# Softmax sums inverted by VectorE block transposes in all attention groups, a third W3 buffer and a new order table

## The chip, the cores and the metric

The kernel runs on one core of a Trainium2 chip. The metric is device time in microseconds (us) of one execution, taken as the median of several runs. The engines are named as in the profile: PE is TensorE (its weight loads are PEld), ACT is ScalarE, DVE is VectorE, POOL is GpSimd, and SP is SyncE, which here issues every DMA. A profile is one further execution, recorded instruction by instruction; its times are counted from the start of its span.

## The reference

The input is x with 2048 rows and 640 columns in bfloat16. Branch A is attention with 32 heads of 20 columns, branch B is a mixer with an MLP, and the second gates the first.

```python
def reference(A_x, A_wqkv, A_wo, B_x, B_w1, B_w2, B_w3, B_w4):
    def _A_ref(x, wqkv, wo):
        B, S, D = x.shape
        H = 32
        Dh = D // H
        ...
        scores = jnp.einsum("bhqd,bhkd->bhqk", q, k) * (Dh ** -0.5)
        p = _softmax(scores, axis=-1)
        o = jnp.einsum("bhqk,bhkd->bhqd", p, v)
        return (lambda x, *d: x.transpose(*d))(o, 0, 2, 1, 3).reshape(B, S, D) @ wo

    def _B_ref(x, w1, w2, w3, w4):
        h = _gelu(_layernorm(x, axis=-1) @ w1)
        ...
        x1 = x + hs
        h2 = _gelu(_layernorm(x1, axis=-1) @ w3) @ w4
        return x1 + h2

    x = A_x
    xn = _layernorm(x, axis=-1)
    s = _A_ref(xn, A_wqkv, A_wo)
    g = _silu(_B_ref(xn, B_w1, B_w2, B_w3, B_w4))
    return x + s * g
```

The hs left out is four shifted quarters of h times w2. What matters for the change is the softmax: exponentials are summed over the keys, and each head's output is divided by its sum.

## The kernel before

**Groups.** The 32 heads are worked in 8 quads of four heads, and each quad in 4 chunks (qc) of 512 queries: 32 groups, called quad_qc. In a group the four heads lie in four strips of 32 partitions. For every tile of 128 keys PE computes scores into PSUM (`score_act`, `score_rows`, `score_both`; their matmuls are L1377, one head's strip of rows each, and L1392, the same scores in column form). ACT takes the exponential of most of them (L1434, 1024 columns at a time, and L1416, 2048 columns). Some score tiles go to DVE instead, which builds exponentials from bits (L1461 takes scores out of PSUM, L1360 makes three shifted copies). PE then multiplies by the values (L1235 for ACT's tiles, L1369 for DVE's) and accumulates the whole group in one PSUM bank, the PV bank. In each strip rows 0 to 19 of that bank are a head's output, and row 20 is its sum of exponentials, since the values carry a column of ones.

**Normalising.** `normalise` (L1468) ends a group. It is written in two forms. In the last quad (three groups; the very last group is worked in two halves by `last_half`) it stays on DVE: a transpose in 32x32 blocks from the PV bank to the buffer Ob (L1483) brings the sums of 16 blocks side by side in each partition, a reciprocal of 16 columns inverts them (L1485), one tensor_tensor multiplies every block by its reciprocal (L1491), and a second block transpose turns the result back (L1493). In the other 7 quads, 28 groups, the sums go through DRAM. DVE copies the PV bank to Ob (L1496). SP stores the sums of the four heads to the DRAM tensor `sums` (L1499) and loads them back spread over 128 partitions into ZT (L1501). DVE inverts them (L1503). SP stores the reciprocals to `recips` (L1505) and loads them back, each row repeated for 32 partitions, into RB (L1507). DVE multiplies Ob by RB into one half of On (L1509). In both of these forms the next group's PV matmuls wait until Ob has been filled. The 28 groups then store their heads with four DMAs to the DRAM tensor `heads` (L1514), from where `otq` fetches them for the output projection.

**Other work.** Between the attention instructions lie the stacks of keys and queries (`stack`, L1104 to L1143: weights, matmuls in `mm_tile`, L640, evictions L1112, stores L1114), the fetches of the next quad (L1133), the masked queries of a group (`qm`, four DMAs at L1202) and branch B. In `b_w34` each of the 4 chunks streams W3 in 12 tiles of 160 KB into W3s (L1795), 48 loads in all. W3s has two buffers, so a tile's load can go only when the tile two before has been used by PE. W4 is loaded in halves (L1809). The two Gelus of this part are single ACT instructions (L1804); a third belongs to `b_w1` (L1733).

**What sets the order.** Each operation is a task (`T`) with its engine, what it reads and what it writes. The order of all tasks is written out in the string TABLE, and `Planner.follow` replays it: two characters give the number of a task, and one more character follows for each set of slots that it takes (PSUM banks, buffers of exponentials). Each engine runs its own tasks in that order, and waits are put where a task reads or writes what another engine's task made or still uses. SP is in order too: a DMA whose wait is not over holds all DMAs behind it. Score tasks made with `flex` choose row or column form by what PE has before and after them in the table, as these lines say:

```python
                nx = next(later)
                if t.flex and (pe_mode or (nx is not None and (nx.mode or nx.flex))):
                    t.mode, t.dur = 1, self.row_dur
```

Of the kernel before, what the change touches and what calls it, by code (L numbers as in the profile page):

```python
# [436 lines left out]
FP32 = mybir.dt.float32  # L437
# [7 lines left out]
class Handle:  # L445
    _n = 0
# [128 lines left out]
class Gen:  # L575
# [71 lines left out]
    def build(self, plan_only=False):  # L647
        nc, pl = self.nc, self.pl
        with contextlib.ExitStack() as es:
# [4 lines left out]
            self.dz, self.dr = (nc.dram_tensor(n, (2, 4, 512), FP32, kind="Internal").ap() for n in ("sums", "recips"))  # L654
# [113 lines left out]
    def alloc_persistent(self):  # L768
# [28 lines left out]
        self.ZT = self.alloc("ZT", [2, 16], FP32)  # L797
        self.RZ = self.alloc("RZ", [2, 16], FP32)
        self.RB = self.alloc("RB", [512], FP32)
# [387 lines left out]
    def attn_quad(self, quad):  # L1187
# [9 lines left out]
        for qc in range(NQC):  # L1197
            seq = cfg.order(quad, qc)
            gb = self.grp % 2
# [47 lines left out]
    def last_half(self, quad, qc, half, gb):  # L1247
# [40 lines left out]
        for x, kt in enumerate(ks):  # L1288
            hs, sa = scores(kt, "a")
            hp, pa = self.exp_act(hs, sa)  # L1290
# [89 lines left out]
    def score_act(self, b, qc, kt, a, gb=None):  # L1380
# [4 lines left out]
        def fn(e):  # L1385
            for jj in range(2):
# [4 lines left out]
                for c in range(4):  # L1391
# [5 lines left out]
                    writes=[sa], name=f"sc{self.step}", mode=int(gb is None), part=a + 1, flex=gb is not None, cls=-1, acq=("S", hs)))  # L1397
        return self.exp_act(hs, sa)

    def score_rows(self, b, qc, kt, wide):  # L1400
# [3 lines left out]
        def fn(e):  # L1404
# [4 lines left out]
          writes=[a for _, a in tiles], name=f"sr{self.step}", mode=1, cls=-1, acq=("SW" if wide else "SR",) + tuple(h for h, _ in tiles))  # L1409
        if not wide:  # L1410
            return [self.exp_act(h, a) for h, a in tiles]
# [6 lines left out]
          reads=[a0, a1], writes=pa, name=f"exp{self.step}", due=self.at(self.nact + 2), acq=("PT2", hp[0], hp[1]), rel=[h0, h1], cls=0)  # L1418
# [10 lines left out]
    def exp_act(self, hs, sa):  # L1429
        cfg = self.cfg  # L1430
        hp = Handle()
        pa = ("PT", hp.id)
        self.T("act", c_act(1024),
               lambda e: e.activation(self.PT[:, hp.slot, :], self.psum[:, 512 * hs.slot:512 * hs.slot + 1024], AF.Exp, scale=cfg.scale),  # L1434
               reads=[sa], writes=[pa], name=f"exp{self.step}", due=self.at(self.nact + 1), acq=("PT", hp), rel=hs)
        self.step += 1
        self.nact += 1
        return hp, pa

    def score_both(self, b, qc, kt, a, quad, r):  # L1440
# [9 lines left out]
        def fn(e):  # L1450
# [5 lines left out]
          name=f"sb{self.step}", mode=1, cls=-1, acq=("SD", hs, hd))  # L1456
        slot = self.exp_act(hs, sa)
# [10 lines left out]
    def normalise(self, quad, qc):  # L1468
# [9 lines left out]
        else:  # L1478
            dst, dsta = self.On[:, ob, :], [A("On", ob)]
        if last:  # L1480
            OnT = self.On[:, ob, :]
            cls = -1
            T("dve", c_dve(512), lambda e: e.transpose(Ob[:, :], self.bank(self.PVB)[:, :]),  # L1483
              writes=[("PV", 0), A("Ob")], name=f"ob{quad}_{qc}", cls=cls)
            T("dve", c_dve(16, "recip"), lambda e: e.reciprocal(RZ[:, ob, 0:16], Ob[:, 20:512:32]),  # L1485
              reads=[A("Ob")], writes=[A("RZ", ob)], name=f"rz{quad}_{qc}", cls=cls)
            def fnn(e):
                in0 = Ob[:, :].rearrange("p (a b) -> p a b", b=32)
                r = RZ[:, ob, 0:16]
                in1 = bass.AP(r.tensor, r.offset, [list(r.ap[0]), [1, 16], [0, 32]])  # L1490
                return e.tensor_tensor(OnT[:, :].rearrange("p (a b) -> p a b", b=32), in0, in1, op=ALU.mult)  # L1491
            T("dve", c_dve(512, "1x"), fnn, reads=[A("Ob"), A("RZ", ob)], writes=[A("On", ob)], name=f"onT{quad}_{qc}", cls=cls)
            T("dve", c_dve(512, "1x"), lambda e: e.transpose(dst, OnT[:, :]), reads=[A("On", ob)], writes=dsta, name=f"on{quad}_{qc}", cls=cls)  # L1493
            return
        ZT, RB = self.ZT, self.RB
        T("dve", c_dve(512), lambda e: e.tensor_copy(Ob[:, :], self.bank(self.PVB)[:, :]),  # L1496
          writes=[("PV", 0), A("Ob")], name=f"ob{quad}_{qc}", cls=-1)
        dz, dr, do = self.dz, self.dr, self.do
# [452 lines left out]
```

## Time and profile before

| what | us |
|---|---|
| median of 3 runs | 866.87 |
| the 3 runs | 865.56, 868.62, 866.87 |
| the profiled execution, device time | 864.35 |
| its span from first to last instruction | 862.6 |
| exponentials on ACT, L1434, 788 instructions | 733.1 |
| score evictions on DVE, L1461, 245 instructions | 264.8 |
| shifted copies on DVE, L1360, 174 instructions | 195.7 |

A row of the groups of instructions names the line, the engine and the operation, then output and input with their shapes, the number of instructions, their busy time in us and the mean length of one in ns, and after a bar the idle time of the engine just before them with what ended it. In the timeline the first two numbers are start and length in us, and square brackets give idle time before the instruction and what ended it. SPq is SP issuing a DMA. The chain of waits follows the work that ended last back to the start, so its shares say through which engine the end was reached.

### The profile page before, as it was taken

What the parts mean: (1) busy time and instruction counts of PE and PEld (TensorE: products, weight loads), DVE (VectorE), ACT (ScalarE), POOL (GpSimd) and SP (SyncE); (2) the same over time, 40 slices, a digit from 0 to 9 for tenths busy, and PEclk for the clock granted to TensorE, in tenths of its full rate; (3) what the DMA queues carried; (4) which work ended last, traced back from release to release, by engine and by line L of the source; (5) the groups of instructions that cost most, each with busy time, mean ns of one, the idle gap of its engine ahead of it and who ended that gap; (6) DMA issues with size and microseconds to landing.
All of it is one profiled execution on the core that took longest, in us unless ns stands there. A gap on an engine that the chain in (4) does not pass through costs nothing.

```text
span 862.6 us, 32161 instructions
## 1 busy us (share of the span) xinstructions
PE 802.2 (93%) x14614; PEld 338.8 (39%) x14614; DVE 719.2 (83%) x1005; ACT 815.6 (95%) x854; POOL 39.2 (5%) x75
## 2 busy tenths in 40 slices
PE   7999999899999999989999999999897899989996
PEld 4433333334345433333434444343233344433475
DVE  7549998998998899979887899988785788997765
ACT  7799999999999999989999999999799999999996
POOL 5610000000000000000000000000000000010000
PEclk9999999999999999999999999999998999999999
DMA  7002453331210023222223121322212102031232
GB/s 230 17 2 65 110 125 107 77 98 47 62 53 17 24 73 89 66 57 63 66 66 86 30 61 41 94 59 79 56 44 57 48 26 71 25 106 63 81 106 79
DMA packets 86472, 58.88 MB, mean 68 GB/s; under 512 B 53056, under 2 KB 77840, under 8 KB 86336
## 3 DMA queue, kind: packets, MB, share of 16 engines
q1 hardware_dynamic: 86336, 56.82, 24.4%
q8 instruction: 115, 1.88, 0.9%
q14 instruction: 21, 0.17, 0.1%
HBM read 42.10 MB, written 10.63 MB: 61 GB/s over the span
## 4 chain that ended last, share of the span: by engine, by line
ACT 46%; PE 35%; DVE 11%; DMA 5%; SPq 2%; issue 1%; DVEq 0%
ACT arena L1434 42%; PE psum L640 13%; PE psum L1392 6%; PE psum L1377 5%; PE psum L1369 4%; DVE arena L1461 4%; PE psum L1235 3%; DMA arena<-in_B_w_dram 3%; DVE arena L1360 2%; PE psum L1276 2%; ACT arena L1804 1%; ACT arena L1733 1%; DMA arena<-sums 1%; ACT arena L1820 1%; DVE arena L855 1%
## 5 line engine op out<-in xcount | busy, mean ns | idle before, releaser
L1434 ACT ACTIVATE arena<-psum 128x1024 bf16<-128x1024 f32 x788 | 733.1, 1041 | 27.9 <-PE psum L1377 19.5
L640 PE MATMUL psum<-arena 128*32 128x320 bf16 (+1 forms) x5952 | 364.8, 334 | 8.6 <-DMA arena<-in_B_w_dram 5.0
L1461 DVE TENSOR_SCALAR arena<-psum 128x1024 uint16<-128x1024 f32 (+1 forms) x245 | 264.8, 1091 | 41.3 <-PE psum L1377 39.7
L640 PEld LDWEIGHTS psum<-arena 128*32 128x32 bf16 x5952 | 147.1, 96 | 145.0 <-issue 32.0
L1360 DVE TENSOR_SCALAR arena<-arena 128x4096 uint16<-128x4096 uint16 (+1 forms) x174 | 195.7, 1149 | 4.0 <-PE psum L1369 2.6
L1392 PE MATMUL psum<-arena 128*32 128x512 bf16 x2496 | 190.5, 382 | 1.5 <-ACT arena L1434 0.8
L1377 PE MATMUL psum<-arena 32*128 32x512 bf16 x1360 | 160.1, 386 | 29.3 <-ACT arena L1434 21.5
L1369 PE MATMUL psum<-arena 128*22 128x512 bf16 x1728 | 152.5, 385 | 5.0 <-DVE arena L1360 4.9
L1235 PE MATMUL psum<-arena 128*22 128x512 bf16 x1552 | 148.0, 382 | 2.5 <-ACT arena L1434 2.4
L1377 PEld LDWEIGHTS psum<-arena 32*128 32x128 bf16 x1360 | 40.9, 91 | 168.8 <-ACT arena L1434 101.0
L1392 PEld LDWEIGHTS psum<-arena 128*32 128x32 bf16 x2496 | 49.2, 95 | 72.0 <-ACT arena L1434 60.0
L1369 PEld LDWEIGHTS psum<-arena 128*22 128x22 bf16 x1728 | 41.7, 92 | 54.8 <-issue 14.6
L1235 PEld LDWEIGHTS psum<-arena 128*22 128x22 bf16 x1552 | 38.7, 91 | 50.1 <-issue 16.1
L1112 DVE CAST arena<-psum 128x512 bf16<-128x512 f32 x40 | 27.2, 686 | 14.7 <-PE psum L640 14.4
L1800 DVE CAST arena<-psum 128x512 bf16<-128x512 f32 x48 | 32.8, 685 | 5.1 <-PE psum L640 5.0
L1584 DVE SCALAR_TENSOR_TENSOR arena<-psum,arena 128x320 bf16<-128x320 f32 x32 | 15.5, 486 | 22.8 <-PE psum L640 22.5
L1174 DVE CAST arena<-psum 128x320 bf16<-128x320 f32 x32 | 15.1, 489 | 15.7 <-PE psum L640 14.4
L855 DVE BATCH_NORM_STATS2 arena<-arena 128x6 f32<-128x320 bf16 x54 | 24.3, 481 | 3.1 <-DMA arena<-in_A_x_dram 3.0
L1815 DVE TENSOR_TENSOR arena<-psum,arena 128x320 bf16<-128x320 f32 x32 | 15.5, 485 | 7.0 <-PE psum L640 6.7
L1804 ACT ACTIVATE arena<-arena 128x12288 bf16<-128x12288 bf16 x2 | 20.9, 10446 | 0.0
L1761 DVE TENSOR_TENSOR arena<-psum,arena 128x320 bf16<-128x320 f32 x32 | 15.2, 481 | 6.8 <-PE psum L640 6.6
L1496 DVE COPY arena<-psum 128x512 f32<-128x512 f32 x28 | 19.1, 682 | 1.1 <-PE psum L929 0.4
(121 smaller groups left out, 347.9 us busy)
## 6 DMA issues: line engine op xcount, KB each, us to landing
arena<-in_B_w_dram SPq DMA_DIRECT2D x48, 160.0 KB, 2.6
arena<-recips SPq DMA_DIRECT2D x28, 256.0 KB
arena<-arena SPq DMA_DIRECT2D x124, 32.0 KB, 1.9
arena<-in_B_w_dram SPq DMA_DIRECT2D x4, 960.0 KB, 6.3
arena<-in_A_x_dram SPq DMA_DIRECT2D x8, 320.0 KB, 6.1
arena<-in_A_x_dram SPq DMA_DIRECT2D x16, 160.0 KB, 2.8
out_dram<-arena SPq DMA_DIRECT2D x16, 160.0 KB, 1.8
heads<-arena SPq DMA_DIRECT2D x112, 20.0 KB
```

Source lines behind the costliest of these rows:

```text
L640: ins = e.matmul(pb[32 * c:32 * c + 32, 0:N], lhsT(k, c), rhs(k, c), start=(k == 0), stop=(stop and k == nk - 1), tile_position=(0, 32 * c))
L855: lambda e, li=li, n=n, hh=hh: e.bn_stats(st[:, li, 6 * hh:6 * hh + 6], xn[:, n, hD * hh:hD * hh + hD]),
L1112: T("dve", c_dve(512), lambda e, h=h, c=c: e.tensor_copy(KS[:, 512 * c:512 * c + 512], self.wbank(h)[:, 0:512]), reads=[wa], writes=[A("KS ...
L1235: ins = e.matmul(pb[32 * i:32 * i + 22, 0:512], VA[:, ql, kts[i // 2], i, :], PT[:, slots[i // 2][0].slot, 512 * (i % 2):512 * (i % 2) + 512],
L1360: T("dve", c_dve(w, "4x"), lambda e, v=v, dst=dst: e.tensor_scalar(dst, U[:, ub, 0:w], EXP_B[v], None, op0=ALU.add), reads=halves, writes= ...
L1369: ins = e.matmul(pb[32 * i:32 * i + 22, 0:512], wv, dst[:, at:at + 512].bitcast(BF16), start=first, stop=final, tile_position=(0, 32 * i))
L1377: return e.matmul(out, self.KT[32 * i:32 * i + 32, b, 128 * kt:128 * kt + 128], self.QT[32 * i:32 * i + 32, b, 512 * qc:512 * qc + 512], s ...
L1392: ins = e.matmul(out[32 * c:32 * c + 32, :], self.KT[:, b, 128 * kt + 32 * c:128 * kt + 32 * c + 32], self.QM[:, gb, 2 * a + jj, :], start ...
L1434: lambda e: e.activation(self.PT[:, hp.slot, :], self.psum[:, 512 * hs.slot:512 * hs.slot + 1024], AF.Exp, scale=cfg.scale),
L1461: ins = e.tensor_scalar(U[:, ub, 1024 * at + 512 * k:1024 * at + 512 * k + w], self.psum[:, 512 * hd.slots[k]:512 * hd.slots[k] + w], a_ex ...
L1800: T("dve", c_dve(512), lambda e, h=h, fc=fc, i=i: e.tensor_copy(GT[:, i, fc, :], self.wbank(h)[:, 0:512]), reads=[wa], writes=at, name=f"g ...
L1804: T("act", 2750 + c_act(2 * FC * 512), lambda e: e.activation(GT[:, :, :, :], GT[:, :, :, :], AF.Gelu_apprx_tanh), reads=gta, writes=gta, ...
```

## The change

All groups now use the form of the last quad. The transposed result of a group needs a buffer of its own: in the 28 groups it is the half of On that the group before used. The DRAM tensors for sums and reciprocals and the buffers ZT and RB are gone, with four DMAs per group. W3s gets a third buffer. TABLE is replaced as a whole, since the numbers of the tasks move; score and exponential tasks also get names made of group, key tile and half, which appear in no instruction.

```diff
-            self.dz, self.dr = (nc.dram_tensor(n, (2, 4, 512), FP32, kind="Internal").ap() for n in ("sums", "recips"))
...
-        self.ZT = self.alloc("ZT", [2, 16], FP32)
         self.RZ = self.alloc("RZ", [2, 16], FP32)
-        self.RB = self.alloc("RB", [512], FP32)
...
+        OnT, ota = (self.On[:, ob, :], A("On", ob)) if last else (self.On[:, 1 - ob, :], A("On", 1 - ob))
+        cls = -1
+        T("dve", c_dve(512), lambda e: e.transpose(Ob[:, :], self.bank(self.PVB)[:, :]),
+          writes=[("PV", 0), A("Ob")], name=f"ob{quad}_{qc}", cls=cls)
+        T("dve", c_dve(16, "recip"), lambda e: e.reciprocal(RZ[:, ob, 0:16], Ob[:, 20:512:32]),
+          reads=[A("Ob")], writes=[A("RZ", ob)], name=f"rz{quad}_{qc}", cls=cls)
+        def fnn(e):
+            in0 = Ob[:, :].rearrange("p (a b) -> p a b", b=32)
+            r = RZ[:, ob, 0:16]
+            in1 = bass.AP(r.tensor, r.offset, [list(r.ap[0]), [1, 16], [0, 32]])
+            return e.tensor_tensor(OnT.rearrange("p (a b) -> p a b", b=32), in0, in1, op=ALU.mult)
+        T("dve", c_dve(512, "1x"), fnn, reads=[A("Ob"), A("RZ", ob)], writes=[ota], name=f"onT{quad}_{qc}", cls=cls)
+        T("dve", c_dve(512, "1x"), lambda e: e.transpose(dst, OnT), reads=[ota], writes=dsta, name=f"on{quad}_{qc}", cls=cls)
         if last:
...
             return
-        ZT, RB = self.ZT, self.RB
-        T("dve", c_dve(512), lambda e: e.tensor_copy(Ob[:, :], self.bank(self.PVB)[:, :]),
-          writes=[("PV", 0), A("Ob")], name=f"ob{quad}_{qc}", cls=-1)
-        dz, dr, do = self.dz, self.dr, self.do
-        T("sp", C_SP, lambda e: e.dma_start(dz[ob], Ob[20:128:32, :]), reads=[A("Ob")], writes=[("dz", ob)], is_dma=True, nbytes=8192,
...
-        T("sp", C_SP, lambda e: e.dma_start(ZT[:, ob, :], dz[ob].rearrange("i (a b) -> (i a) b", b=16)), reads=[("dz", ob)],
...
-        T("dve", c_dve(16, "recip"), lambda e: e.reciprocal(RZ[:, ob, :], ZT[:, ob, :]),
...
-        T("sp", C_SP, lambda e: e.dma_start(dr[ob].rearrange("i (a b) -> (i a) b", b=16), RZ[:, ob, :]), reads=[A("RZ", ob)],
...
-        T("sp", C_SP, lambda e: e.dma_start(RB[:, :], bass.AP(dr.tensor, dr[ob].offset, [[512, 4], [0, 32], [1, 512]])),
...
-        T("pool" if cfg.ONP else "dve", 1500 if cfg.ONP else c_dve(512, "1x"), lambda e: e.tensor_tensor(dst, Ob[:, :], RB[:, :], op=ALU.mult),
...
+        do = self.do
...
-        self.W3s = self.alloc("W3s", [2, KC, 128], BF16)
+        self.W3s = self.alloc("W3s", [3, KC, 128], BF16)
...
-                ws = self.w3k % 2
+                ws = self.w3k % 3
```

## The prediction

> **What bounds the kernel now.** I read the page's totals first, then busy time by stretch, then the chain of waits, then the timeline around its longest DMA pieces.
>
> ```profile
> span 862.6 us, 32161 instructions
> PE 802.2 (93%) x14614; PEld 338.8 (39%) x14614; DVE 719.2 (83%) x1005; ACT 815.6 (95%) x854; POOL 39.2 (5%) x75
> ...
> ACT 46%; PE 35%; DVE 11%; DMA 5%; SPq 2%; issue 1%; DVEq 0%
> ```
>
> ScalarE (ACT) is the bound: 815.6 of 862.6 us busy, so all its idle time is 47 us, and no change that leaves its work alone can gain more. The third line, the chain that ended last, still passes through DVE for 11% and DMA for 5%. The stretches say where the idle 47 us lie (columns: length, then busy us of PE, PEld, DVE, ACT, POOL):
>
> ```profile
> 0.00:44.00 44.00, 37.98 (x858) 19.61 (x862) 29.54 (x99) 32.82 (x53) 26.47 (x50) 1.00 0.42 121
> 44.00:160.00 116.00, 109.88 (x1714) 39.49 (x1706) 96.71 (x119) 110.59 (x119) 2.80 (x7) 1.00 0.33 84
> 160.00:300.00 140.00, 133.14 (x2452) 56.71 (x2452) 124.11 (x193) 137.86 (x139) 2.90 (x6) 1.00 0.19 52
> 300.00:450.00 150.00, 142.82 (x2402) 54.38 (x2398) 134.46 (x176) 144.43 (x144) 4.07 (x9) 1.00 0.26 66
> 450.00:650.00 200.00, 187.70 (x3310) 76.24 (x3310) 173.09 (x207) 191.71 (x205) 0.00 (x0) 0.99 0.25 63
> 650.00:760.00 110.00, 101.68 (x1870) 43.90 (x1862) 88.69 (x105) 107.79 (x104) 0.00 (x0) 0.97 0.16 44
> 760.00:863.00 103.00, 89.00 (x2040) 48.49 (x2036) 72.63 (x112) 90.37 (x95) 2.94 (x3) 0.96 0.29 91
> ```
>
> Start and end hold 11.2 and 12.6 us, and the change leaves the work of both alone. The middle, 44 to 760, where the 28 changed groups run, holds 5.4 + 2.1 + 5.6 + 8.3 + 2.2 = 23.6 us of ACT idle. That is what can be won there. DVE is busy 617 of these 716 us: 99 us are free, but all in pieces.
>
> The largest single piece of ACT idle in the middle starts on the SP queue:
>
> ```profile
> 603.47 0.34 SPq L1505 DMA_DIRECT2D recips<-arena  x1
> 606.78 0.59 SPq L1507 DMA_DIRECT2D arena<-recips  x1
> 607.42 10.82 SPq L1795 DMA_DIRECT2D arena<-in_B_w_dram  x3
> ...
> 612.82 0.68 PE L640 MATMUL psum<-arena 128*32 128x512 bf16 x8 [2.59 <-DMA arena<-in_B_w_dram]
> ...
> 614.40 1.02 ACT L1434 ACTIVATE arena<-psum 128x1024 bf16<-128x1024 f32 x1 [3.04 <-PE psum L1392]
> ```
>
> SP works in order. It sends the reciprocals out (L1505, 603.47) and waits until they are in DRAM before it fetches them back (L1507, 606.78). The W3 tile (L1795) queued behind leaves only at 607.42 and is awaited by PE, which stands for 2.59 us; ACT runs dry 3.04 us. The same order (L1507 at 375.87, L1795 at 376.51) precedes a PE stop of 1.58 us at 381.69 and an ACT gap of 1.66 us at 383.43.
>
> [...] 8 KB from L1501 or L1505 lands after 2.2 us in the median, and L1507 held SP for 41.7 us in all waiting for L1505's data. [...] L1509 takes 682, L1491 688. [...] the last quad's transposes, 705 and 706 ns, cost about what the 682 ns copy of the same size does. So every new DVE operation has a measured row.
>
> **The change, part by part.** All sums are made against the profiled span, 862.6 us; its own time was 864.35 and the median of the three others is 866.87, so I apply the difference to 866.87.
>
> 1. DVE. The old group is L1496 + L1503 + L1509, the new one L1483 + L1485 + L1491 + L1493, which quad 7 already runs:
>
> ```profile
> L1496 DVE COPY arena<-psum 128x512 f32<-128x512 f32 x28 | 19.1, 682 | 1.1 <-PE psum L929 0.4 <-PE psum L1369 0.3
> L1509 DVE TENSOR_TENSOR arena<-arena 128x512 bf16<-128x512 f32 x28 | 19.1, 682 | 0.0
> L1503 DVE RECIPROCAL arena<-arena 128x16 f32<-128x16 f32 x28 | 6.8, 244 | 3.1 <-DMA arena<-sums 3.1
> ...
> L1483 DVE STREAM_TRANSPOSE arena<-psum 128x512 f32<-128x512 f32 x3 | 2.1, 706 | 0.0
> L1493 DVE STREAM_TRANSPOSE arena<-arena 128x512 bf16<-128x512 bf16 x3 | 2.1, 705 | 0.0
> ...
> L1491 DVE TENSOR_TENSOR arena<-arena 128x512 bf16<-128x512 f32 x3 | 2.1, 688 | 0.1
> ...
> L1485 DVE RECIPROCAL arena<-arena 128x16 f32<-128x16 f32 x3 | 0.7, 247 | 0.1
> ```
>
> Old 682 + 244 + 682 = 1608 ns, new 706 + 247 + 688 + 705 = 2346 ns: 738 ns more, x28 = 20.7 us. The PV bank comes free only 24 ns later (706 against 682). What of 20.7 us lies on the path? Lower end: weight each stretch's groups by DVE's share of the chain there. The chain asked by stretch shows DVE 18.6% (44 to 160, 4 groups), 0 (160 to 300, 6), 8.3% (300 to 450, 5.5), 1.2% (450 to 650, 8.5), 8.6% (650 to 770, 4): 1.65 groups x 0.738 = 1.2 us. Upper end: all, 20.7. A delay off the chain also uses up slack of what follows, so I take three times the lower end, **+3.5 us**.
>
> 2. The trips. Each group loses L1499, L1501, L1505, L1507, 112 DMAs in all, with their SP issue (541 + 350 + 345 + 588 ns = 1.8 us a group) and the waits in front of them. On DVE, L1503 had waited 3.1 us in three stops (100.23, 460.16, 712.02). The first was followed by ACT gaps of 0.80 and 0.76 (102.06, 103.85), the last by 0.21 (713.61), the second by none: **-1.8 us**. I take nothing for the other SP relief (qm, fetch, rstd loads): mostly it lies beside ACT work; between 44 and 160, SP and issue are 11.7% of the chain, so up to 2 us are possible.
>
> 3. W3s with three buffers. I read both tables with the rule of follow(): two characters name a task, then one per slot set taken; the ids of the new one are the old ones with four tasks per group taken out and onT put in. In the old SP order 22 of 48 W3 loads stand directly behind one of the four trip DMAs, in the new none. Issue to first use was 3 ACT tasks at the least and 5 or 6 typically, and exps follow each other every 0.92 us (47 in 43.38 us from 45.49); now it is 5 at the least and 10 typically. A W3 load lands after 2.6 us (median; at most 6.2). So I let the W3 gaps vanish: ACT 1.66 + 3.04 + 0.81 (616.23) + 0.20 (617.45) = **-5.7 us**. The chain's other W3 pieces (4.95 us at 556.52, 2.48 at 570.57) left 0.19 and no ACT idle, so I count nothing. The W4 load on it (6.78 at 450.97) gets no buffer more.
>
> 4. The order. The three Gelus start at the same place on ACT in both (after 206, 418 and 640 ACT tasks), and W1, W2, W3 and Silu begin within a few. So it is the same plan shifted, not another. PE gets 12 fewer flexible score tiles in column form (312 to 300; L1392's 2496 matmuls are 312 x 8). A column tile takes about 0.44 us of PE (372.06 to 372.50), a row tile about half of 0.32: 12 x 0.28 = 3.4 us of PE, of which PE's 35% of the chain makes **-1.0 us**; bounds 0 and 3.4.
>
> 5. A new wait. onT writes the other half of On, so it waits until the previous group's four head stores (L1514) have read it. Behind it on DVE stand score evictions (L1461) for which PE waits. In the new table 5 to 30 exps lie between those stores and onT; even 5 are 4.6 us, against 1.3 us of issue and about 2 us of landing. I take 0; if SP comes late in the two tightest places, 2 us. Renamed tasks cost nothing: they emit no instruction.
>
> Sum: 3.5 - 1.8 - 5.7 - 1.0 = -5.0; 866.87 - 5.0 = **862 us**, 0.6% faster. Own range: -2.6 to -9, 858 to 864.3.
>
> **Rivals.**
> A. Hidden anyway: the W3 and sums gaps were slack used once; with them gone ACT meets the next limit (PE, 93%). Half of 7.5 gained, DVE at 4: 866.87 - 3.75 + 4 = 867. For it: of 17.8 us of W3 loads on the chain only 5.7 idled ACT. Against it: PE itself stood still 2.59 us.
> B. DVE becomes the bound. Each group puts two 0.7 us operations more or less ahead of the L1461 evictions, on which PE already waited 4.8 us; DVE was busy 43.3 of 44 us between 301 and 345. It decides once more than 8.5 of the 20.7 us (41%) land on the path. If all groups but the 6 of the ACT-bound 160 to 300 pay in full: 22 x 0.738 = 16.2, less 7.5: 876 us, slower.
> C. More than counted: without trips the whole schedule fits, half of the other 16 us of ACT idle in the middle goes too, and DVE costs 1.2: 866.87 - 7.5 - 8 + 1.2 = 852.6.
> The change could also fail to do what it says: a third buffer doesn't help a load that SP issues late. The new SP order speaks against it.
>
> **How the numbers follow.** Forecast 0.50, C 0.14, A 0.12, B 0.24. A measurement of this kernel tells 0.3%, 2.6 us, from no change. Faster 0.50 + 0.14 = 0.64, same 0.12, slower 0.24. The range of 8 in 10 leaves out C's last part and the upper half of B: 852 to 873.
>
> **What would show it.** After the change: no DMA of sums or recips; DVE busy near 719 + 21 = 740; ACT busy unchanged near 816 and its idle in 44 to 760 near 18; no PE idle put down to in_B_w_dram above 1 us; SP's waits shorter. If B holds, ACT's and PE's waits for L1461 or the normalising lines rise by more than 8 us. I am wrong if ACT idle in the middle exceeds 23.6, or if it falls while start or end grows.

## The result and the profile after

| | before | after |
|---|---|---|
| median of 4 runs, us | 867.05 | 861.16 |
| lowest and highest, us | 865.56, 868.62 | 860.99, 861.55 |
| the profiled execution, device time and span, us | 864.35, 862.6 | 861.55, 859.6 |

The ratio after to before is 0.9933, 95% interval 0.9914 to 0.9951: 5.8 us less, between 4.2 and 7.5. The forecast was 862. The two spans differ by only 3.0 us, because the profiled execution of before was 2.7 us quicker than the median of its kernel, while that of after was 0.4 us slower than its own. A comparison of the two traces line by line therefore sees half of the gain.

The page of after, with busy time of each engine and the chain that ended last:

```profile
span 859.6 us, 31925 instructions
PE 800.6 (93%) x14542; PEld 338.8 (39%) x14542; DVE 734.7 (85%) x1031; ACT 815.5 (95%) x854; POOL 39.3 (5%) x75
...
ACT 63%; PE 29%; DVE 7%; issue 1%; DMA 1%; SPq 0%; DVEq 0%
```

ScalarE does the same work (815.5 against 815.6 us). DVE has 15.5 us more to do and still falls from 11% of the chain to 7%. DMA falls from 5% to 1%. The chain runs along ACT for 63% instead of 46%. After is nearer to a pure ACT bound.

The stretches of after (columns: length, then busy us of PE, PEld, DVE, ACT and POOL, then granted clock, DMA share and GB/s):

```profile
0.00:44.00 44.00, 38.36 (x832) 19.48 (x832) 29.35 (x97) 31.50 (x51) 26.05 (x50) 0.96 0.41 122
44.00:160.00 116.00, 110.49 (x1714) 39.68 (x1712) 99.19 (x122) 111.85 (x121) 3.19 (x9) 1.00 0.28 74
160.00:300.00 140.00, 132.50 (x2430) 56.48 (x2428) 126.23 (x193) 137.42 (x139) 3.34 (x6) 1.00 0.15 43
300.00:450.00 150.00, 142.46 (x2354) 53.89 (x2354) 138.48 (x187) 144.77 (x144) 4.37 (x8) 0.99 0.22 52
450.00:650.00 200.00, 188.86 (x3370) 76.65 (x3358) 183.24 (x224) 196.22 (x206) 0.34 (x1) 1.00 0.22 54
650.00:760.00 110.00, 103.39 (x1904) 45.29 (x1904) 90.76 (x107) 108.73 (x110) 0.09 (x1) 0.98 0.11 29
760.00:860.00 100.00, 84.56 (x1966) 47.38 (x1962) 67.48 (x106) 85.00 (x89) 1.89 (x3) 0.95 0.29 90
```

Length less ACT busy is ACT's idle time. From 44 to 760 it is 4.2 + 2.6 + 5.2 + 3.8 + 1.3 = 17.0 us, where before had 23.6. Most of that is in 450 to 650 (8.3 to 3.8), one of the two stretches in which W3 is streamed. The start grew from 11.2 to 12.5 us. The end grew too: from the last exponential to the end of the span it is 11.0 us instead of 8.3.

The groups of after (busy us, mean ns, then idle time before them):

```profile
L640 PE MATMUL psum<-arena 128*32 128x320 bf16 (+1 forms) x5952 | 359.2, 335 | 0.6 <-DVE arena L1459 0.2
...
L1480 DVE STREAM_TRANSPOSE arena<-psum 128x512 f32<-128x512 f32 x31 | 21.9, 708 | 1.7 <-PE psum L1367 1.2 <-PE psum L1233 0.2
L1490 DVE STREAM_TRANSPOSE arena<-arena 128x512 bf16<-128x512 bf16 x31 | 21.8, 702 | 0.2
L1488 DVE TENSOR_TENSOR arena<-arena 128x512 bf16<-128x512 f32 x31 | 21.1, 680 | 0.1
L1482 DVE RECIPROCAL arena<-arena 128x16 f32<-128x16 f32 x31 | 7.5, 240 | 0.2
```

The four operations cost what the prediction took from quad 7 (708, 240, 680 and 702 ns against 706, 247, 688 and 705). DVE stood 0.1 us ahead of the multiplication, L1488, in all 31 groups together, so the new wait for the head stores costs nothing. And L640 has lost its waits: now it stands 0.6 us and no DMA is named, where before it stood 8.6 us:

```profile
L640 PE MATMUL psum<-arena 128*32 128x320 bf16 (+1 forms) x5952 | 364.8, 334 | 8.6 <-DMA arena<-in_B_w_dram 5.0 <-DVE arena L1174 1.4 <-DVE arena L1461 1.1
```

So nearly every sign that the prediction asked for is there. What the traces can't tell is whose doing it is: four things were changed at once. The experiments take them apart.

### The profile page after: what moved, and what is told of

It reads as the page before. It is cut to its first block, busy times and chain, and to the rows that moved or that the text cites. A ratio compares the mean times of both kernels' runs of the same rounds, so it can differ in the third digit from the quotient of the medians.

```text
span 859.6 us, 31925 instructions
## 1 busy us (share of the span) xinstructions
PE 800.6 (93%) x14542; PEld 338.8 (39%) x14542; DVE 734.7 (85%) x1031; ACT 815.5 (95%) x854; POOL 39.3 (5%) x75
## 4 chain that ended last, share of the span: by engine, by line
ACT 63%; PE 29%; DVE 7%; issue 1%; DMA 1%; SPq 0%; DVEq 0%
ACT arena L1432 57%; PE psum L640 10%; PE psum L1375 5%; PE psum L1390 4%; PE psum L1367 3%; PE psum L1233 3%; DVE arena L1459 2%; ACT arena L1787 2%; PE psum L1274 1%; ACT arena L1803 1%; DVE arena L1358 1%; ACT arena L1414 1%; ACT arena L1716 1%; DVE arena L852 1%; PE psum L963 1%
## 5 line engine op out<-in xcount | busy, mean ns | idle before, releaser
L1432 ACT ACTIVATE arena<-psum 128x1024 bf16<-128x1024 f32 x788 | 733.1, 1039 | 20.8 <-PE psum L1375 17.8
L640 PE MATMUL psum<-arena 128*32 128x320 bf16 (+1 forms) x5952 | 359.2, 335 | 0.6 <-DVE arena L1459 0.2
L1459 DVE TENSOR_SCALAR arena<-psum 128x1024 uint16<-128x1024 f32 (+1 forms) x243 | 263.7, 1094 | 31.8 <-PE psum L1375 30.5
L640 PEld LDWEIGHTS psum<-arena 128*32 128x32 bf16 x5952 | 148.8, 97 | 132.6 <-issue 31.2
L1375 PE MATMUL psum<-arena 32*128 32x512 bf16 x1384 | 165.6, 387 | 34.6 <-ACT arena L1432 24.2
L1358 DVE TENSOR_SCALAR arena<-arena 128x4096 uint16<-128x4096 uint16 (+1 forms) x174 | 194.7, 1142 | 2.9 <-PE psum L1367 1.8
L1390 PE MATMUL psum<-arena 128*32 128x512 bf16 x2400 | 182.7, 381 | 3.1 <-ACT arena L1432 2.1
L1233 PE MATMUL psum<-arena 128*22 128x512 bf16 x1552 | 148.9, 383 | 2.4 <-ACT arena L1432 2.0
L1367 PE MATMUL psum<-arena 128*22 128x512 bf16 x1728 | 146.2, 381 | 3.3 <-DVE arena L1358 3.1
L1375 PEld LDWEIGHTS psum<-arena 32*128 32x128 bf16 x1384 | 42.0, 91 | 179.5 <-ACT arena L1432 115.1
L1390 PEld LDWEIGHTS psum<-arena 128*32 128x32 bf16 x2400 | 46.1, 95 | 69.3 <-ACT arena L1432 57.7
L1367 PEld LDWEIGHTS psum<-arena 128*22 128x22 bf16 x1728 | 40.6, 91 | 53.6 <-issue 15.5
L1233 PEld LDWEIGHTS psum<-arena 128*22 128x22 bf16 x1552 | 38.8, 91 | 49.9 <-issue 18.6
L1783 DVE CAST arena<-psum 128x512 bf16<-128x512 f32 x48 | 32.7, 681 | 3.0 <-PE psum L640 2.5
L1567 DVE SCALAR_TENSOR_TENSOR arena<-psum,arena 128x320 bf16<-128x320 f32 x32 | 15.5, 489 | 22.5 <-PE psum L640 22.3
L1171 DVE CAST arena<-psum 128x320 bf16<-128x320 f32 x32 | 15.1, 486 | 16.2 <-PE psum L640 16.0
L1480 DVE STREAM_TRANSPOSE arena<-psum 128x512 f32<-128x512 f32 x31 | 21.9, 708 | 1.7 <-PE psum L1367 1.2
L1490 DVE STREAM_TRANSPOSE arena<-arena 128x512 bf16<-128x512 bf16 x31 | 21.8, 702 | 0.2
L1744 DVE TENSOR_TENSOR arena<-psum,arena 128x320 bf16<-128x320 f32 x32 | 15.1, 480 | 7.2 <-PE psum L640 7.0
L1488 DVE TENSOR_TENSOR arena<-arena 128x512 bf16<-128x512 f32 x31 | 21.1, 680 | 0.1
```

Source lines behind the costliest of these rows:

```text
L640: ins = e.matmul(pb[32 * c:32 * c + 32, 0:N], lhsT(k, c), rhs(k, c), start=(k == 0), stop=(stop and k == nk - 1), tile_position=(0, 32 * c))
L1233: ins = e.matmul(pb[32 * i:32 * i + 22, 0:512], VA[:, ql, kts[i // 2], i, :], PT[:, slots[i // 2][0].slot, 512 * (i % 2):512 * (i % 2) + 512],
L1358: T("dve", c_dve(w, "4x"), lambda e, v=v, dst=dst: e.tensor_scalar(dst, U[:, ub, 0:w], EXP_B[v], None, op0=ALU.add), reads=halves, writes= ...
L1367: ins = e.matmul(pb[32 * i:32 * i + 22, 0:512], wv, dst[:, at:at + 512].bitcast(BF16), start=first, stop=final, tile_position=(0, 32 * i))
L1375: return e.matmul(out, self.KT[32 * i:32 * i + 32, b, 128 * kt:128 * kt + 128], self.QT[32 * i:32 * i + 32, b, 512 * qc:512 * qc + 512], s ...
L1390: ins = e.matmul(out[32 * c:32 * c + 32, :], self.KT[:, b, 128 * kt + 32 * c:128 * kt + 32 * c + 32], self.QM[:, gb, 2 * a + jj, :], start ...
```

## The experiments

All ratios are to the kernel before on the same chip, with a 95% interval. "Old order" means that the order table of before is kept, with the tasks that fall away taken out and onT put directly ahead of the final transpose. 1% of the time is 8.7 us.

| run | what it is | median us | ratio | interval |
|---|---|---|---|---|
| norm_only | new normalising, old order, two W3 buffers | 869.96 | 1.0027 | 1.0012 to 1.0042 |
| both_old | the same with three W3 buffers | 869.95 | 1.0026 | 1.0012 to 1.0041 |
| w3_two | after with two W3 buffers | 862.26 | 0.9934 | 0.9910 to 0.9959 |
| trips_out | before without the four trip DMAs | 857.36 | 0.9881 | 0.9856 to 0.9906 |
| trips_out_dve | trips_out with one more DVE transpose a group | 869.72 | 1.0052 | 1.0035 to 1.0069 |
| trips_pool | before, trip DMAs issued by POOL | 860.91 | 0.9924 | 0.9900 to 0.9948 |
| trips_unread | before, trips made but read by nobody | 863.32 | 0.9971 | 0.9957 to 0.9985 |
| dose_plus | after with one more DVE transpose a group | 870.55 | 1.0027 | 1.0012 to 1.0041 |
| dose_minus | after without the final transpose | 862.11 | 0.9932 | 0.9909 to 0.9956 |
| mult_pool | after, multiplication on POOL | 862.04 | 0.9939 | 0.9917 to 0.9961 |
| norm_spread | norm_only, multiplication placed earlier | 865.24 | 1.0000 | 0.9982 to 1.0018 |
| norm_pool_old | old order, multiplication on POOL | 857.10 | 0.9905 | 0.9885 to 0.9925 |

### The third W3 buffer: both_old against norm_only, w3_two against after

norm_only takes the normalising of after and undoes the rest:

```diff
-        self.W3s = self.alloc("W3s", [3, KC, 128], BF16)
+        self.W3s = self.alloc("W3s", [2, KC, 128], BF16)
...
-                ws = self.w3k % 3
+                ws = self.w3k % 2
```

with the old order in TABLE. both_old leaves those two lines as after has them. w3_two makes the same edit to after; 38 of its 48 loads move back in SP's order, to where the second buffer is free.

> The change's normalising form in all groups, W3s with two buffers, and the order of the kernel before: the trips' tasks are taken out of its table and the added multiplication stands directly ahead of the final transpose, at the place of the old multiplication. Theory (the sum of the prediction, DVE +3.5, stops on the sums -1.8, W3 loads no longer queued behind trips some -4 of -5.7): about -2.3, 864.7 us. Rival 'the new table made the gain': the extra DVE time alone is felt, 868 to 872 us. Rival 'DVE costs most of its 20.7 us and bigger SP gains hide it': 867 us or more, with ACT idle put down to PE and DVE up by over 5 us.

> The whole change except for its order: normalising form and third W3s buffer, with the order of the kernel before as in the run above. Theory: 3.5 - 1.8 - 5.7 = -4.0, 863 us, so the new order is worth 2 us. Rival 'the new table made the gain': 867 us or slower. If the third buffer does more than the trips' end, this is 3 us or more below the run with two buffers; if the end of the trips frees the loads already, within 1 us of it.

> The changed kernel with two W3s buffers; 38 of its W3 loads are moved back in the order to just behind the last matmul of the tile two before. Theory: the trips were what made W3 loads late, so this loses 1 to 2 us against the changed kernel, 862 to 863 us. Rival 'the third buffer is the gain': the W3 gaps come back, +5.7, 867 us, with PE idle put down to the W3 load of 4 us or more.

With the trips gone, the buffer is worth nothing in either order: 1.0026 against 1.0027, and 0.9933 against 0.9934. What it would do while the trips are still there was not run. Yet the gaps that it was meant to close are closed without it. The waits of norm_only, all that name a weight of branch B (total us, times, longest):

```profile
PE psum L640 <- DMA arena<-in_B_w_dram: 1.1, 2, 0.6
PEld psum L640 <- DMA arena<-in_B_w_dram: 1.1, 1, 1.1
```

And those of before:

```profile
PE psum L640 <- DMA arena<-in_B_w_dram: 5.0, 5, 2.6
PEld psum L640 <- DMA arena<-in_B_w_dram: 3.8, 2, 3.1
```

(PE and PEld can stand for the same transfer, so the two aren't added up.) The SP queue of norm_only at the place that corresponds to the largest gap of before:

```profile
596.08 1.62 SPq L1497 DMA_DIRECT2D heads<-arena  x4
597.74 0.40 SPq L1792 DMA_DIRECT2D arena<-in_B_w_dram  x1
601.84 19.82 SPq L1778 DMA_DIRECT2D arena<-in_B_w_dram  x6
```

Six W3 loads (L1778) leave one after the other with nothing between them. In before a store and a fetch of reciprocals stood among the loads here, and the next load waited until 607.42 for them. So what kept these tiles late was not the lack of a buffer, it was what stood ahead of their loads in the queue; trips_pool below tests that by itself.

### What the trips cost: trips_out, trips_pool, trips_unread

```diff
+        T("dve", 200, lambda e: e.memset(self.RB[:, :], 0.001), writes=[A("RB")], name="rb_one")
+        T("dve", 60, lambda e: e.memset(self.ZT[:, :, :], 1000.0), writes=[A("ZT", 0), A("ZT", 1)], name="zt_one")
...
-        T("sp", C_SP, lambda e: e.dma_start(dz[ob], Ob[20:128:32, :]), reads=[A("Ob")], writes=[("dz", ob)], is_dma=True, nbytes=8192,
...
-        T("sp", C_SP, lambda e: e.dma_start(RB[:, :], bass.AP(dr.tensor, dr[ob].offset, [[512, 4], [0, 32], [1, 512]])),
```

trips_out leaves out the division by the sums in 28 groups and keeps DVE's work; all four DMAs go.

> The kernel before without the four DMAs of each trip: the reciprocal reads a buffer filled once with a constant, and the multiplication reads another constant, so the division by the softmax sums is left out in 28 groups; all DVE operations and the order stay. This is the price of the trips alone. Theory: stops on the sums -1.8 and most of the W3 gaps, -4 to -5.7: 859.5 to 861.5 us. Rival 'the trips were hidden': 866 to 867 us.

It gains 10.3 us (8.1 to 12.5), more than the 7.5 that the prediction counted for trips and W3 gaps together. ACT's idle time between 300 and 650, where W3 is streamed, falls from 13.9 to 7.5 us, and the weights of branch B keep PE waiting for 0.6 us.

trips_pool makes the same trips from POOL's queue:

```diff
-        T("sp", C_SP, lambda e: e.dma_start(dz[ob], Ob[20:128:32, :]), reads=[A("Ob")], writes=[("dz", ob)], is_dma=True, nbytes=8192,
+        T("pool", C_SP, lambda e: e.dma_start(dz[ob], Ob[20:128:32, :]), reads=[A("Ob")], writes=[("dz", ob)], is_dma=True, nbytes=8192,
```

and so for the other three.

> The kernel before with the four DMAs of each trip issued on POOL's queue instead of SP's: nothing of the computation, of the DVE work or of the order changes, only SP no longer stands in front of W3, qm and fetch loads while a trip is under way. If the 10.3 us that the trips cost were SP's blocking, most of them come back: 858 to 860 us. If they were the stops of DVE on the sums and the DMA traffic, this stays within 3 us of the kernel before, 865 to 868 us.

That alone gains 6.6 us (4.5 to 8.7). Its waits:

```profile
POOL arena L1501 <- DMA sums<-arena: 57.1, 28, 5.4
POOL arena L1507 <- DMA recips<-arena: 53.7, 28, 4.8
DVE arena L1503 <- DMA arena<-sums: 4.0, 4, 1.9
PE psum L640 <- DMA arena<-in_B_w_dram: 3.7, 5, 1.6
```

POOL now stands for 57.1 + 53.7 us until a store has landed, and nothing of worth is behind it. DVE still waits 4.0 us for sums. Of PE's 3.7 us for weights of branch B, 1.6 are for a half of W4; for W3 (L1795) 2.1 us are left of 4.8, and the longest stop is 0.78 us, where before had 1.58 and 2.59. So moving the trips away from the loads, with two buffers, closes most of the W3 gaps. They are a part of the 6.6 us; that the other loads and stores behind the trips on SP hold the rest is likely, but one profile doesn't split it further.

trips_unread is the counterpart. SP makes all trips with all waits (it stands 50.4 us for the reciprocals, L1503, and stood 52.2 in before), but nobody reads what they bring; DVE takes the reciprocal of other values and a maximum of Ob with itself, so the division is left out here too.

```diff
-        T("dve", c_dve(16, "recip"), lambda e: e.reciprocal(RZ[:, ob, :], ZT[:, ob, :]),
+        T("dve", c_dve(16, "recip"), lambda e: e.reciprocal(RZ[:, ob, :], self.VE[:, 0:16]),
...
-        T("pool" if cfg.ONP else "dve", 1500 if cfg.ONP else c_dve(512, "1x"), lambda e: e.tensor_tensor(dst, Ob[:, :], RB[:, :], op=ALU.mult),
+        T("pool" if cfg.ONP else "dve", 1500 if cfg.ONP else c_dve(512, "1x"), lambda e: e.tensor_tensor(dst, Ob[:, :], Ob[:, :], op=ALU.max),
```

> The kernel before with all its trips still issued by SP with their waits, but nobody reads what they bring: the reciprocal is taken of other values and the multiplication is replaced by a maximum of Ob with itself, so the division by the sums is left out in 28 groups. DVE has the same operations, and can't stop for a trip. Moving the trips to POOL gave back 6.5 of the 10.3 us. If the rest is DVE's stops, this is 3 to 4 us below the kernel before, 863 to 865 us. If the DVE stops cost little and SP's blocking is all, within 1.5 us of the kernel before, 866 to 868 us.

It gains 2.5 us (1.3 to 3.7), near the 1.8 that the prediction gave DVE's stops, and keeps PE's waits for branch B's weights (5.4 and 3.9 us). SP's blocking, 6.6, and DVE's stops, 2.5, make 9.1 of the 10.3; with intervals of some 2 us to either side, that can't be told from the whole. Most of what the trips cost, they cost others in the queue.

### What DVE's added work costs: norm_only against trips_out, trips_out_dve, dose_plus, dose_minus

norm_only has no trips either, but the new DVE work in place of the old. Both ran on the same chip: 869.96 against 857.36, so the DVE work costs 12.6 us in the old order. trips_out_dve adds to trips_out, whose division it also leaves out, nothing but one transpose in each of the 28 groups (the multiplication then writes the other half of On, as in after):

```diff
...
+        OnT = self.On[:, 1 - ob, :]
+        T("dve", c_dve(512, "1x"), lambda e: e.tensor_tensor(OnT, Ob[:, :], RB[:, :], op=ALU.mult),
+          reads=[A("Ob"), A("RB")], writes=[A("On", 1 - ob)], name=f"onT{quad}_{qc}")
+        T("dve", c_dve(512, "1x"), lambda e: e.transpose(dst, OnT), reads=[A("On", 1 - ob)], writes=dsta, name=f"on{quad}_{qc}", lock=True)
```

> The kernel before without the trips' DMAs, as above (constants in place of the reciprocals, so the division is left out), with the old copy at a group's end, but with one block transpose more in each of 28 groups, directly behind the multiplication (the heads then lie transposed in blocks). Theory 'in the old order DVE time itself is the price': 705 of 738 ns, so nearly the whole step from 857.4 to 870, 867 to 870 us. Rival 'the price lies in the new form, its transpose out of PSUM or the wait for the previous group's head stores': clearly less, 858 to 863 us.

From 0.9881 to 1.0052 is 14.8 us for 28 x 0.70 = 19.7 us of instructions. It isn't something special in the new normalising: a plain transpose of this length at this place costs as much. Where it lands is seen in the waits. Three lines each, the first of trips_out:

```profile
PEld psum L1378 <- DVE arena L1462: 37.1, 86, 1.0
ACT arena L1435 <- PE psum L1378: 17.8, 36, 2.0
PE psum L1378 <- DVE arena L1462: 4.0, 11, 0.7
```

and of norm_only, where the same lines are numbered three lower:

```profile
PEld psum L1375 <- DVE arena L1459: 49.0, 95, 1.5
ACT arena L1432 <- PE psum L1375: 23.3, 47, 1.5
PE psum L1375 <- DVE arena L1459: 12.3, 27, 1.1
```

L1459 takes scores out of PSUM so that PE can go on with row scores, L1375. PE waits 8.3 us more for its evictions, and ACT 5.5 us more for PE; trips_out_dve shows the same, with 12.0 us for PE and 23.9 us for ACT. That is the path of rival B, at the size that it named as its sign ("more than 8 us"), though counted from trips_out and not from before.

In the new order one DVE transpose more or less a group was tried on after. dose_plus:

```diff
-        T("dve", c_dve(512, "1x"), lambda e: e.transpose(dst, OnT), reads=[ota], writes=dsta, name=f"on{quad}_{qc}", cls=cls)
+        def fno(e):
+            if not last:
+                e.transpose(Ob[:, 0:256].bitcast(BF16), OnT)
+            return e.transpose(dst, OnT)
+        T("dve", c_dve(512, "1x"), fno, reads=[ota], writes=dsta + ([] if last else [A("Ob")]), name=f"on{quad}_{qc}", cls=cls)
```

dose_minus leaves out the transpose back in 28 groups, as its multiplication writes straight to dst:

```diff
-        T("dve", c_dve(512, "1x"), lambda e: e.transpose(dst, OnT), reads=[ota], writes=dsta, name=f"on{quad}_{qc}", cls=cls)
...
+            T("dve", c_dve(512, "1x"), fnn, reads=[A("Ob"), A("RZ", ob)], writes=dsta, name=f"on{quad}_{qc}", cls=cls)
```

> The changed kernel with one more block transpose (some 0.70 us, into Ob, which nobody reads any more) directly ahead of the final one in each of the 28 groups: 19.7 us more DVE work, in an order that doesn't know of it. Theory 'the old order was the one that could not take more DVE work, the new one leaves room': a fifth to a third of it shows, +4 to +6.5 us on 861.2, 865 to 868 us. Rival 'any order loses 0.6 us per us of DVE work': +12 us, 873 us.

> The changed kernel without the final block transpose in 28 groups: the multiplication stands in its place and writes the heads' half of On directly, so that the back-transposition of each 32x32 block is left out. 19.7 us less DVE work. Theory 'room in the new order': -2 to -5 us, 856 to 859 us. Rival 'any order loses 0.6 us per us of DVE work': -12 us, 849 us.

The price is not a line. Taking 19.7 us of DVE instructions away from after gains nothing that shows (0.9932 against 0.9933, each known to some 2 us); adding as much costs 8.1 us (1.0027), between the expectation and its rival. The waits of after, then of dose_plus:

```profile
PEld psum L1375 <- DVE arena L1459: 40.6, 88, 1.6
ACT arena L1432 <- PE psum L1375: 17.8, 35, 0.9
PE psum L1375 <- DVE arena L1459: 8.3, 16, 1.3
```

```profile
PEld psum L1375 <- DVE arena L1459: 43.9, 87, 1.9
ACT arena L1432 <- PE psum L1375: 24.1, 48, 1.4
PE psum L1375 <- DVE arena L1459: 11.2, 22, 1.6
```

In dose_minus they are 38.9, 18.5 and 7.8 us: hardly less than in after. (The profile of dose_plus is the longest of its executions, 873.08 us against a median of 870.55, so its waits may be somewhat too long.) The new order has room for the new DVE work and not for one more operation of 0.7 us a group; the old order had no room even for the new work. One rival stands: dose_plus puts its transpose next to another one, and norm_spread below says that the place counts too. The extra transpose was not tried elsewhere.

### What the order is worth

both_old is after in all but the order: 1.0026 against 0.9933, so the order gains 8.1 us. PE's waits for L1459 are those of norm_only in both_old, 12.3 us, and ACT's are a little longer, to be held against those of after above:

```profile
ACT arena L1432 <- PE psum L1375: 25.0, 48, 2.3
```

The order turns a change that made the kernel 2.3 us slower into one that makes it 5.8 us faster. But with little DVE work the new order is no better than the old one: dose_minus (0.9932, DVE busy 719.9 us) stands against trips_out (0.9881, 719.6 us), and their intervals don't meet. There it loses 4.4 us. Some of that is at the end. The timeline of the end of before, DVE only (start, length):

```profile
854.67 0.45 DVE L1331 STREAM_TRANSPOSE arena<-psum 128x256 f32<-128x256 f32 x1
855.05 0.79 DVE L1603 SCALAR_TENSOR_TENSOR arena<-psum,arena 128x640 bf16<-128x640 f32 x1
855.76 0.18 DVE L1333 RECIPROCAL arena<-arena 128x8 f32<-128x8 f32 x1
...
856.95 0.44 DVE L1340 STREAM_TRANSPOSE arena<-arena 128x256 bf16<-128x256 bf16 x1
```

and of after, with the two PE lines that matter:

```profile
847.75 1.39 PE L640 MATMUL psum<-arena 128*32 128x320 bf16 x34
...
849.89 0.28 PE L1264 MATMUL psum<-arena 128*22 128x256 bf16 x2
...
850.21 0.45 DVE L1329 STREAM_TRANSPOSE arena<-psum 128x256 f32<-128x256 f32 x1
850.59 0.79 DVE L1586 SCALAR_TENSOR_TENSOR arena<-psum,arena 128x640 bf16<-128x640 f32 x1
851.41 0.49 DVE L1628 TENSOR_TENSOR arena<-arena 128x640 bf16<-128x640 bf16 x1
...
852.39 0.82 DVE L1586 SCALAR_TENSOR_TENSOR arena<-psum,arena 128x640 bf16<-128x640 f32 x1
853.24 0.49 DVE L1628 TENSOR_TENSOR arena<-arena 128x640 bf16<-128x640 bf16 x1
853.65 0.44 DVE L1338 STREAM_TRANSPOSE arena<-arena 128x256 bf16<-128x256 bf16 x1
```

The last exponential ends at 854.27 in before and at 848.57 in after. The last half group's normalising (L1331 to L1340, now L1329 to L1338) must then reach its final transpose before the last output projection can start. In before that transpose starts 2.7 us after the exponential, in after 5.1 us. The new order lets other work of the last rows go first, in two places. On PE, matmuls of L640 run ahead of the last products with the values (L1264), which end at 850.17, so that the normalising begins 1.6 us after the exponential instead of 0.4. On DVE, two of L1586 and two of L1628 then stand between its steps (in before the same operations are L1603 and L1645, one and two of them), and it takes 3.4 us instead of 2.3. From last exponential to end is 8.3 to 8.4 us in all profiles of the old order that were read for it and 10.8 to 11.0 in those of the new one. This is read from timelines; no run with the end alone put back was made.

There is a rival for all of the 4.4 us: the granted clock, the share of its full speed that TensorE was granted in the mean of an execution. It is lower with the new order (medians 0.985 to 0.988 over the runs of after, w3_two, dose_plus, dose_minus and mult_pool, against 0.990 to 0.994 for the old one). And in before the executions with a lower clock are mostly the longer ones. Of 43 on one chip, 7 at 0.988 have a median of 870.0 us, 15 at 0.990 one of 868.3 and 4 at 0.994 one of 864.4. By the last two, 3.9 us for 0.004, the 0.0075 between trips_out (0.993) and dose_minus (0.9855) would be some 7 us, an estimate. So it isn't shown that the new order is worse as an order, even with little DVE work. By the same estimate its 8.1 us against both_old (0.992, after 0.988) would be some 4 us more at an equal clock. No run held the clock, and why the new order has less of it is not known.

### Placing and moving the multiplication: mult_pool, norm_spread, norm_pool_old

mult_pool gives the multiplication of the 28 groups in after to POOL:

```diff
-        T("dve", c_dve(512, "1x"), fnn, reads=[A("Ob"), A("RZ", ob)], writes=[ota], name=f"onT{quad}_{qc}", cls=cls)
+        T("dve" if last else "pool", c_dve(512, "1x"), fnn, reads=[A("Ob"), A("RZ", ob)], writes=[ota], name=f"onT{quad}_{qc}", cls=cls)
```

> The changed kernel with the multiplication by the reciprocals (L1488) moved to POOL in 28 groups: 19 us less DVE work, but one more hop between two engines. If DVE time is what the change pays with, this is -2 to -5 us, 856 to 859 us. If the hop or POOL's access to memory beside DVE costs more, at or above 861 us, with longer DVE instructions beside the POOL ones.

The groups of mult_pool:

```profile
L1488 POOL TENSOR_TENSOR arena<-arena 128x512 bf16<-128x512 f32 x28 | 35.2, 1257 | 555.4 <-DVE arena L1482 530.7 <-DVE arena L1065 24.7
...
L1490 DVE STREAM_TRANSPOSE arena<-arena 128x512 bf16<-128x512 bf16 x31 | 21.7, 701 | 1.3 <-POOL arena L1488 1.2
```

POOL takes 1257 ns in the mean where DVE takes 680. Its median is 1048 ns, 1.54 times DVE's 680, and 8 of the 28 are longer, 1.36 to 1.93 us. Those 8, and no others, start while DVE is busy with a shifted copy (L1358). The copies are longer too, as the expectation's rival has it, but little: those of 4096 columns take 1236 ns in the mean instead of the 1216 of after, and the copies of both sizes together 197.5 us instead of 194.7. DVE waits 1.2 us for POOL in all. The time doesn't move (0.9939), as dose_minus leads one to think: in the new order DVE work between 720 and 735 us costs nothing that shows.

norm_spread is norm_only with the multiplication half-way between the reciprocal and the final transpose in DVE's order, instead of directly ahead of the transpose; it differs from norm_only in TABLE alone. norm_pool_old is norm_spread with the edit of mult_pool.

> The change's normalising form with the old order and two W3s buffers, as above, but the multiplication stands half-way between reciprocal and final transpose in DVE's order, not directly ahead of the transpose. If the old order lost by two operations of 0.7 us in a row ahead of score evictions, 2 to 5 us less than 870, 865 to 868 us. If the amount of DVE work is what counts, 869 to 871 us.

> The change's normalising form with the old order and two W3s buffers, but with the multiplication by the reciprocals on POOL in 28 groups, half-way between reciprocal and final transpose: DVE then has 706 + 245 + 702 = 1653 ns a group, 45 ns more than the kernel before, and no trips. If the trips' 10.3 us and the DVE time's 12.6 us in the old order add up as measured, this is 10.3 - 12.6 x 45/738 = 9.5 us below the kernel before, 857.5 to 859 us, faster than the changed kernel. If POOL's 1.26 us and the hop hold DVE up, 862 us or more.

norm_spread is level with before, 1.0000, some 2.3 us better than norm_only, though the intervals of the two overlap a little. PE's waits for L1459 agree, 7.2 us instead of 12.3. So it is likely, rather than shown, that two DVE operations of 0.7 us side by side hurt more than the same two apart. norm_pool_old reaches 857.1 us, 8.2 us less than before, the least of all versions that do the whole work. Its interval (0.9885 to 0.9925) overlaps that of after (0.9914 to 0.9951), so that it beats after is likely rather than shown. It has the old order, two W3 buffers and no trips. Its DVE is busy for 720.7 us, its POOL for 73.7.

## Why the prediction was right, and by which steps

The total was right, 861.2 against 862, by luck: two large errors cancel. Each part measured with runs of the old order first:

| step | predicted us | measured us | by |
|---|---|---|---|
| 1 DVE work | +3.5 | +12.6 | norm_only less trips_out |
| 2 and 3 trips and W3 gaps | -7.5 | -10.3 | trips_out less before |
| 3 third buffer itself | part of the -5.7 | 0 | both_old less norm_only |
| 4 order | -1.0 | -8.1 | after less both_old |
| 5 new wait | 0 | 0 | idle time of L1488 |
| sum | -5.0 | -5.8 | |

The measured column is a walk from before to after, so it must sum to the result. In another sequence its terms would be others, since the parts depend on each other: with little DVE work the new order shows no gain.

**Step 1 failed.** Its durations were right. What failed was "weight each stretch's groups by DVE's share of the chain there", and then three times that. The shares are also read too low. 18.6, 8.3, 1.2 and 8.6% are L1461 and L1360 alone; all DVE lines on the chain have 29.3, 12.8, 2.1 and 15.1% of these stretches. That makes 2.7 groups and 2.0 us, and three times that 5.9 us (three times 1.2 would have been 3.6, not 3.5). Read in full, the rule still gives less than half of what came. The chain shows what lies on one path of the old schedule, and not what delays do on paths that are only a little shorter. With DVE busy for 83% and PE waiting for its evictions, 12.6 of 20.7 us came through, 61%, above the 41% from which rival B decides. B was priced at 16.2 us and is the right story for the old order: norm_only is slower than before. The upper bound of 20.7 held, and trips_out_dve shows that a large part of it can indeed be charged. A lesser slip: DVE was to be busy for 740 us and is for 734.7. Busy time counts each moment once, and neighbours on DVE overlap a little, as this part of after's timeline shows:

```profile
547.09 0.69 DVE L1488 TENSOR_TENSOR arena<-arena 128x512 bf16<-128x512 f32 x1
547.70 1.22 DVE L1459 TENSOR_SCALAR arena<-psum 128x1024 uint16<-128x1024 f32 x1
548.83 0.68 DVE L1783 CAST arena<-psum 128x512 bf16<-128x512 f32 x1
```

L1488 ends at 547.78 and L1459 starts at 547.70; L1459 ends at 548.92 and L1783 starts at 548.83. So 0.08 to 0.09 us of each instruction's length lie over the next here. Over all instructions of DVE, the lengths added up exceed the busy time by 57.8 us in before and by 59.5 in after. The 1.7 us between them are a part of the 5.2 us by which 734.7 falls short of the forecast; the rest was not traced.

**Step 2** was right in kind and a little small: DVE's stops 2.5 us where 1.8 were counted. **Step 3** had the right mechanism in its own evidence (SP "waits until they are in DRAM", with W3 "queued behind") and near its size: trips_out removes 6.4 us of ACT idle in the W3 stretches, where 5.7 were counted. It gave the credit to the third buffer, which has none. In the trace of before the fetches L1507 held SP for 41.7 us in all until the 8 KB stores of L1505 had landed, which took 2.2 us in the median. From that one could expect that removing the waiting DMA frees the loads behind it with two buffers as well, and norm_only shows it; trips_pool put a number to the wait, 6.6 us for the same DMAs on another queue. Of the remaining 2.8 us, DVE's stops make 0.7. Whether "I take nothing for the other SP relief" left out the rest is not shown.

**Step 4 failed** by 7.1 us, nearly as much as step 1 with 9.1, the other way. "So it is the same plan shifted, not another" rested on where Gelus and Silu stand on ACT. That says nothing of where the evictions L1459 stand on DVE among the new operations, and the new table changes that. In norm_only L1488 and L1490 follow one another directly in all 28 groups, in after in 4 only. PE's waits for L1459 fall from 12.3 (both_old) to 8.3 us and ACT's waits for L1375 from 25.0 to 17.8. How much of the 8.1 us is this spacing is open; norm_spread, which spaces them in the old order, gained 2.3. The 12 column tiles that the step did price came as forecast (2400 matmuls of L1390 instead of 2496), but PE's busy time fell by only 2.4 us from both_old to after.

**Step 5 was right**: 0.1 us. Its "about 2 us of landing" for the head stores is an estimate; the 8 KB transfers took 2.2 us in the median. In before the one fetch that stood waiting for head stores (L1566) leaves 1.06 us after the end of the last one's issue (787.64 + 1.48 = 789.12, and 790.18).

**Signs.** ACT's middle idle of 17.0 us (near 18), the vanished waits for branch B's weights and ACT's unchanged 815.5 us came as written. The warning sign came too: "if it falls while start or end grows". The end grew by 2.7 us through the new order, which the prediction took as leaving the end alone. The start grew by 1.3 us, and its first exponential begins anywhere between 31.9 and 34.9 us in the profiles of this study, so that is not the change's.

## What to carry to other kernels

When a transfer arrives late, look at what stands ahead of its issue in the queue and which wait that has, before giving it another buffer: here four small dependent DMAs a group cost 6.6 us by standing there, and with them gone the extra buffer gained 0. Work added to an engine that is 83% busy and feeds the bound is not priced by its share of the chain: 20 us of it cost 12.6 to 14.8 us in one order and nothing that shows in another, and 20 us more cost 8.1 again, so find how much room the order has before counting on it. And a re-planned order is a part of a change with its own price, positive in one place (8.1 us here) and negative in another (2.7 us at the end); take it apart from the rest by running the old order with the new operations, and compare the granted clocks before calling the rest its price.

## What was not expected of the hardware

The block transpose takes the same time for 128x512 in bf16 from SBUF (702 ns) as for float32 from PSUM (708 ns). The same four DMAs a group that hold SP up for 62.5 us in before, by its waits for sums (20.8) and recips (41.7), make POOL stand for 111 us (57.1 + 53.7) in trips_pool, in a kernel that gains 6.6 us by it. A POOL multiplication of 128x512 that starts during one of DVE's shifted copies (L1358) takes up to 1.93 us instead of 1.05: all 8 such of 28 in mult_pool are longer (1.36 to 1.93 us), and all 6 such in norm_pool_old (1.89 to 1.90), where the other 42 of both take 1.05 to 1.10. And executions of before on one chip differ by some 4 us in the median between a granted clock of 0.990 (868.3 us) and one of 0.994 (864.4 us).
